# Packed values first, mixed weights copied out of PSUM, the value by halves of the heads, and another order of the block products in the last entry

## The chip, the cores and the metric

The kernel runs on one core of a Trainium2 chip. The metric is the time of one execution on the device in microseconds (us); lower is better. Before the change three runs took 408.6, 409.43 and 409.56 us.

## The reference, cut to what matters

Two softmax attentions over 8 batch entries (8 heads, 576 positions, head size 64, 32 packed queries), then a gated feed-forward block with a spatial matrix. All data is float32.

```
scale = 1.0 / np.sqrt(q.shape[-1])
def sm_attn(qq, kk, vv):                  # softmax(scale * qq @ kk^T) @ vv
    ...
p_packed = sm_attn(p, k, v)               # 32 packed rows per head
out = sm_attn(q, p_packed, p_packed)      # 576 rows per head
x = out with the heads side by side       # (8, 576, 512)
h = np.maximum(x @ w_in, 0.0)             # 1024 columns
u, v = h[..., :512], h[..., 512:]
v_n = (v - mean(v)) / np.sqrt(var(v) + 1e-06)
v_s = np.einsum('ts,bsd->btd', w_spatial, v_n) + b_spatial[None, :, None]
result = (u * v_s) @ w_out
```

## The kernel before

The eight batch entries are worked off one after the other; the code for entry 0 is written out by hand with the preparation of the weights, and entries 1 to 7 run through one loop over `b`, which is unrolled. The program order of every engine is the order of the code (all calls of TensorE, VectorE, ScalarE and GpSimd are pinned), so an instruction that waits holds up all behind it on its engine. Float32 products are made from a high and a low part (names ending in `_h`, `_l`): the high part is a copy on ScalarE, the low part a subtraction on VectorE, and TensorE adds three products.

PSUM is used as four quarters of two banks, `ps0` to `ps3`, through `on(q0)` to `on(q3)`; each stage takes the quarters in a written order, and a quarter can be written again once its reader is done. One entry on TensorE has these stages, in this order:

- `value(g)`: x @ w_in for the second half of the columns (the normalised half), in three groups of rows. The attention weights `a_h`, `a_l` are multiplied with the mixed weights `m_h[:, 1]`, `m_l[:, 1]` (packed values times w_in); `r` is the half of the heads (parity of the head).
- transposes of the packed weights of entry b+2 and of the packed values of entry b+1.
- `up(e)`: the first half of the columns, four groups.
- the mixing stage, small tiles of the array, work for later entries: `query_scores` (qT,ppT: scores of b+1), `mix(1)` and `mix(0)` (w_in_sb,ppT: mixed weights of b+1), `pack_values` (v_sb,p1T: packed values of b+2) and `pack_scores` (kT,pT: packed scores of b+3). VectorE takes the scores of b+1 out of PSUM by `query_spread`; `mix_hi` and `mix_lo` read the mixed weights in PSUM.
- `gate(e)`: the spatial matrix times the normalised half, four groups of 28 matmuls; `gated(e)` multiplies it into `u` on VectorE.
- `product`: the last matrix product in seven block products of 12 matmuls each (A11, S1, A12, S4, S3, S2, A22), with blocks T1 to T4 formed on VectorE from blocks of `u`. ScalarE makes the high parts (`block_hi`), VectorE the low ones (`block_lo`). P1, P5, P57 and U are sums kept in SBUF.

Between these VectorE and ScalarE run the softmax of entry b+1 (`query_max` to `query_tail`), whose weights the next `value` needs. The four output blocks of an entry are formed in tiles `o` (a pool of two buffers, which also holds `part` of `relu(2)`) and stored by DMAs that SyncE issues. Queue of the loads on SyncE: q of b+2, v of b+3, k of b+4, each behind the stage that read the buffer.

The quoted lines are the end of the last entry: VectorE forms the block 21 in two halves, then 22, each stored by its own DMA.

```
        ff.product(A22, "T4", onto=S3)
...
            for f in range(2):
                ff.out21(slice(f, f + 1))
            ff.out22()
```

## Time and profile before

| | |
|---|---|
| median of three runs | 409.43 us |
| profiled execution, its own time | 407.98 us |
| its span, first to last instruction | 406.2 us |
| busy: PE (matmul), DVE (VectorE), ACT (ScalarE), POOL (GpSimd) | 394.9, 332.9, 192.7, 74.1 us |
| granted TensorE clock, mean | 0.996 of full speed |

A busy PE is not PE at its peak: matmuls overlap, and their ends are modelled. How fast PE really goes is read from the starts of its rows in the timeline. In the trace all instructions carry one line (a helper's), so they are told apart by the names of their tiles: `qT,ppT`, `w_in_sb,ppT`, `v_sb,p1T` and `kT,pT` are the mixing stage, `m_h,a_h` is the value, `wsp` the gates, `wout` the block products.

### The profile page before, as it was taken

What the parts mean: (1) busy time and instruction counts of PE and PEld (TensorE: products, weight loads), DVE (VectorE), ACT (ScalarE), POOL (GpSimd) and SP (SyncE); (2) the same over time, 40 slices, a digit from 0 to 9 for tenths busy, and PEclk for the clock granted to TensorE, in tenths of its full rate; (3) what the DMA queues carried; (4) which work ended last, traced back from release to release, by engine and by line L of the source; (5) the groups of instructions that cost most, each with busy time, mean ns of one, the idle gap of its engine ahead of it and who ended that gap; (6) DMA issues with size and microseconds to landing.
All of it is one profiled execution on the core that took longest, in us unless ns stands there. A gap on an engine that the chain in (4) does not pass through costs nothing.

```text
span 406.2 us, 8936 instructions
## 1 busy us (share of the span) xinstructions
PE 394.9 (97%) x3800; PEld 354.5 (87%) x3800; DVE 332.9 (82%) x567; ACT 192.7 (47%) x291; POOL 74.1 (18%) x98
## 2 busy tenths in 40 slices
PE   7999999999999999999999999999999999999993
PEld 5768977799799879999699888999799889999993
DVE  2597799979799779977899788995899789978563
ACT  3587865766435353434634273244634272526140
POOL 1566445644000120002100030001200030004000
PEclk9999999999999999999999999999999999999998
DMA  7999057730810227020530205002300200020002
GB/s 306 382 383 397 20 178 305 241 116 2 293 66 31 87 81 278 2 85 34 224 129 31 87 13 225 0 29 89 120 0 30 87 2 2 0 102 17 2 30 88
DMA packets 16620, 46.62 MB, mean 115 GB/s; under 512 B 1346, under 2 KB 10562, under 8 KB 13764
## 3 DMA queue, kind: packets, MB, share of 16 engines
q1 hardware_dynamic: 16580, 46.05, 31.1%
q8 instruction: 30, 0.49, 0.5%
q14 instruction: 10, 0.08, 0.1%
HBM read 36.61 MB, written 9.44 MB: 113 GB/s over the span
## 4 chain that ended last, share of the span: by engine, by line
PE 94%; DVE 3%; POOL 1%; issue 1%; DMA 1%; POOLq 0%; DVEq 0%
PE ps_t L43 94%; DVE nmax L43 1%; POOL bits L43 1%; DMA out_t<-o 1%; DVE bits L43 0%; DVE t L43 0%; DVE o L43 0%; DVE sm_t L43 0%; DVE w_in_sb L43 0%; DVE pp L43 0%; DVE mx L43 0%; DVE prod L43 0%; POOL ident masks.py:199 0%; DVE rtot L43 0%; POOL ident masks.py:197 0%
## 5 line engine op out<-in xcount | busy, mean ns | idle before, releaser
L43 PE MATMUL ps_t<-wsp_h,v_h 128*128 128x288 f32 x256 | 55.9, 300 | 0.0
L43 PE MATMUL ps_t<-wsp_l,v_h 128*128 128x288 f32 x256 | 54.5, 295 | 0.0
L43 POOL TENSOR_TENSOR rstd<-mv,eps 128x2 f32<-128x2 f32 (+2 forms) x26 | 6.9, 265 | 245.5 <-DVE mv L43 245.4
L43 PE MATMUL ps_t<-t,wout_h 128*128 128x288 f32 x232 | 48.3, 294 | 0.0
L43 PEld LDWEIGHTS ps_t<-wsp_h,v_h 128*128 128x128 f32 x256 | 40.8, 188 | 3.8 <-DVE m_l L43 1.9
L43 PEld LDWEIGHTS ps_t<-wsp_l,v_h 128*128 128x128 f32 x256 | 41.5, 189 | 0.0
L43 ACT CAST g_h<-u 128x576 fp32r<-128x576 f32 x24 | 16.1, 674 | 49.4 <-DVE u L43 49.1
L43 PE MATMUL ps_t<-wsp_h,v_l 128*128 128x288 f32 x256 | 39.4, 296 | 0.0
L43 PEld LDWEIGHTS ps_t<-t,wout_h 128*128 128x128 f32 x232 | 38.0, 188 | 0.0
L43 PEld LDWEIGHTS ps_t<-wsp_h,v_l 128*128 128x128 f32 x256 | 35.9, 189 | 0.5 <-issue 0.5
L43 PE MATMUL ps_t<-t,wout_l 128*128 128x288 f32 x116 | 32.3, 294 | 0.0
L43 PE MATMUL ps_t<-g_h,wout_h 128*128 128x288 f32 x104 | 30.1, 305 | 0.6 <-DVE pp L43 0.6
L43 PE MATMUL ps_t<-g_h,wout_l 128*128 128x288 f32 x104 | 29.1, 295 | 0.0
L43 PE MATMUL ps_t<-a_h,m_h 128*128 128x288 f32 x128 | 28.1, 301 | 0.0
L43 PE MATMUL ps_t<-a_h,m_l 128*128 128x288 f32 x128 | 27.4, 296 | 0.0
L43 PE MATMUL ps_t<-a_l,m_h 128*128 128x288 f32 x128 | 27.4, 296 | 0.0
L43 DVE TENSOR_TENSOR u<-ps_t,u 128x576 f32<-128x576 f32 x28 | 21.0, 749 | 7.3 <-PE ps_t L43 7.3
L43 PE MATMUL ps_t<-m_l,a_h 128*128 128x512 f32 x80 | 25.8, 390 | 0.0
L43 PE MATMUL ps_t<-m_h,a_h 128*128 128x512 f32 x80 | 25.8, 391 | 0.0
L43 ACT ACTIVATE sm_t<-sm_t 128x576 f32<-128x576 f32 x16 | 11.0, 685 | 27.5 <-DVE sm_t L43 23.7
L43 DVE TENSOR_TENSOR o<-ps_t,prod 128x576 f32<-128x576 f32 (+1 forms) x15 | 10.7, 717 | 15.4 <-DMA out_t<-o 15.1
L43 ACT COPY part<-ps_t 64x512 f32<-64x512 f32 x8 | 4.7, 583 | 39.2 <-DVE o L43 39.2
(136 smaller groups left out, 989.6 us busy)
## 6 DMA issues: line engine op xcount, KB each, us to landing
out_t<-o SPq DMA_DIRECT2D x31, 288.0 KB, 2.3
v_sb<-in_v SPq DMA_DIRECT2D x8, 1024.0 KB, 8.1
qT<-in_q SPq DMA_DIRECT2D x7, 1152.0 KB, 5.4
kT<-in_k SPq DMA_DIRECT2D x7, 1152.0 KB, 8.4
raw<-in_w_in SPq DMA_DIRECT2D x4, 1024.0 KB, 12.7
raw<-in_w_out SPq DMA_DIRECT2D x2, 1024.0 KB, 9.8
kT<-in_k SPq DMA_DIRECT2D x2, 576.0 KB
qT<-in_q SPq DMA_DIRECT2D x2, 576.0 KB, 12.8
```

The lines of the kernel that those rows point to most:

```text
L43: return lambda *a, **k: self.tc.keep_in_program_order(call(*a, **k))
```

## The change

Four parts. (1) In the mixing stage `pack_values` and `packed` move ahead of `query_scores`, and the two `mix` follow each other. `mix_keep` copies each mixed-weight result whole from PSUM to SBUF (tile `kept`) on ScalarE, and `mix_hi` and `mix_lo` read the copy; `mix_lo(1)` moves behind the packed maxima of b+3. The load of v stands before that of q on SyncE. The quarters are dealt out anew. (2) `value(2)` and `value(0)` run by halves of the heads, first half of both, then second half of both. (3) The block products move to `down` and `last_down`. In `down` (entries 1 to 6) the products keep their order, and the work of VectorE and ScalarE between them is reordered: the sums and the scaling of the second softmax half (`query_sum(1)`, `query_norm(1)`) move from before the last gate into the products. Blocks 22 and 21 are formed in place in `prod` tiles (P57 and U) and stored from there. (4) `last_down` (entry 7) orders the products A11, S1, S2, S3, S4, A22, A12; the block 11 comes last, copied by ScalarE and stored in two halves.

```diff
@@ -487,6 +487,12 @@
                         True,
                     )
 
+        def mix_keep(self, x):
+            kept = two.tile([P, 2, FH], F32, tag="vn", name="kept")
+            act.copy(kept, self.ms[x])
+            self.ms[x] = kept
         def mix_hi(self, x, rs=slice(0, 2)):
             act.copy(self.m_h[:, x, rs, :], self.ms[x][:, rs, :])
 
@@ -510,7 +516,7 @@
         def chunks(self, g):
             return [c for c in (2 * g, 2 * g + 1) if c <= NC]
 
-        def value(self, g, psum=None, js=(0, 1), ns=(0, 1, 2)):
+        def value(self, g, psum=None, js=(0, 1), ns=(0, 1, 2), rs=(0, 1)):
             a_h, a_l, m_h, m_l = (getattr(self.att, x) for x in ("a_h", "a_l", "m_h", "m_l"))
             if g not in self.ps:
                 self.ps[g] = psum()
@@ -521,7 +527,7 @@
             if self.b == 0:
                 steps.sort(key=lambda rn: rn[1])
             for r, n in steps:
-                if n not in ns:
+                if n not in ns or r not in rs:
                     continue
                 aa, ww = terms[n]
                 for i in js[: len(self.chunks(g))]:
@@ -768,6 +774,12 @@
             act.copy(o, self.ds[k][:, :, :HS])
             self.put(o, f, t)
 
+        def out11_split(self):
+            o = self.out_block()
+            for i in range(2):
+                act.copy(o[:, i], self.ds[A12][:, i, :HS])
+                self.put(o, 0, 0, slice(i, i + 1))
         def out11(self):
             self.out_whole(A12, 0, 0)
 
@@ -776,16 +788,84 @@
             self.add_part(o, "U", S4)
             self.put(o, 0, 1)
 
-        def out21(self, fs=slice(0, 2)):
-            if fs.start == 0:
-                self.o21 = self.out_block()
-            self.add_part(self.o21, "U", A22, fs)
-            self.put(self.o21, 1, 0, fs)
+        def out21(self):
+            o = self.part("U")
+            self.add_part(o, "U", A22)
+            self.put(o, 1, 0)
 
         def out22(self):
-            o = self.out_block()
-            dve.tensor_tensor(o, self.part("U"), self.part("P57"), op=ALU.add)
+            o = self.part("P57")
+            dve.tensor_tensor(o, self.part("U"), o, op=ALU.add)
             self.put(o, 1, 1)
+        def down(self, turns, nxt):
+            self.product(A11, "g11", psum=on(turns[0]))
+            self.block_hi("g21")
+            self.block_sum("T3")
+            self.block_hi("T3")
+            self.block_lo("g21")
+            self.keep_part("P1", A11)
+            self.block_sum("T2")
+            self.block_hi("g22")
+            self.product(S1, "T1", psum=on(turns[1]))
+            self.block_lo("g22")
+            self.block_lo("T3")
+            self.block_hi("T2")
+            nxt.query_sum(1)
+            self.keep_part("P5", S1)
+            self.product(A12, "g21", onto=A11)
+            self.out11()
+            self.block_lo("T2")
+            nxt.query_norm(1)
+            self.block_sum("T4")
+            self.block_hi("T4")
+            self.product(S4, "g22", onto=S1)
+            nxt.query_turn(1)
+            nxt.query_hi(1)
+            self.product(S3, "T3", psum=on(turns[2]))
+            self.add_part("P57", "P5", S3)
+            self.block_lo("T4")
+            nxt.query_lo(1)
+            nxt.query_tail(1)
+            self.product(S2, "T2", psum=on(turns[3]))
+            self.add_part("U", "P1", S2)
+            self.out12()
+            self.product(A22, "T4", onto=S3)
+            self.out22()
+            self.out21()
+        def last_down(self, turns):
+            self.product(A11, "g11", psum=on(turns[0]))
+            self.block_sum("T2")
+            self.block_hi("T2")
+            self.block_sum("T3")
+            self.block_hi("T3")
+            self.block_lo("T2")
+            self.keep_part("P1", A11)
+            self.product(S1, "T1", psum=on(turns[1]))
+            self.block_hi("g22")
+            self.block_lo("T3")
+            self.block_lo("g22")
+            self.keep_part("P5", S1)
+            self.block_sum("T4")
+            self.block_hi("T4")
+            self.product(S2, "T2", psum=on(turns[3]))
+            self.add_part("U", "P1", S2)
+            self.block_hi("g21")
+            self.product(S3, "T3", psum=on(turns[2]))
+            self.block_lo("T4")
+            self.add_part("P57", "P5", S3)
+            self.block_lo("g21")
+            self.product(S4, "g22", onto=S1)
+            self.out12()
+            self.out22()
+            self.product(A22, "T4", onto=S3)
+            self.out21()
+            self.product(A12, "g21", onto=A11)
+            self.out11_split()
 
 
 
@@ -1109,8 +1189,9 @@
         att, nxt, far = nxt, far, further
         further = Attention(b + 3) if b + 3 < B else None
         ff = FeedForward(b, att)
-        ff.value(2, psum=on(q0))
-        ff.value(0, psum=on(q1))
+        for r in range(2):
+            ff.value(2, psum=on(q0), rs=(r,))
+            ff.value(0, psum=on(q1), rs=(r,))
         ff.relu(2)
         ff.value(1, psum=on(q2))
         ff.relu(0)
@@ -1146,42 +1227,45 @@
         ff.up(3, psum=on(q3))
         ff.up_relu(3)
         ff.norm_hi(1)
+        if far:
+            far.pack_values(on(q1))
+            far.packed()
+            if further:
+                load_v(b + 3)
         if nxt:
-            nxt.query_scores(psum=by_turns(q1, q2))
+            s0, s1, m1, m0 = (q2, q0, q3, q1) if far else (q1, q2, q0, q3)
+            nxt.query_scores(psum=by_turns(s0, s1))
             nxt.query_tiles()
             if far:
                 load_q(b + 2)
-            nxt.mix(1, psum=on(q0))
             nxt.query_spread(0)
+            nxt.mix(1, psum=on(m1))
+            nxt.mix_keep(1)
             nxt.query_spread(1)
+            nxt.mix(0, psum=on(m0))
+            nxt.mix_keep(0)
             nxt.mix_hi(1)
-            if far:
-                far.pack_values(on(q3))
-                far.packed()
-                if further:
-                    load_v(b + 3)
-            nxt.mix_lo(1)
         ff.norm_lo(1)
         if nxt:
-            nxt.mix(0, psum=on(q1))
-            nxt.mix_hi(0)
             if further:
-                further.pack_scores(psum=by_turns(q2, q3))
+                further.pack_scores(psum=by_turns(s0, s1))
                 if b + 4 < B:
                     load_k(b + 4)
                 for r in range(2):
                     further.pack_max(r)
                     further.pack_exp(r)
-            nxt.mix_lo(0)
+            nxt.mix_lo(1)
+            nxt.mix_hi(0)
             nxt.query_max(0)
             nxt.query_sub(0)
             nxt.query_exp(0)
+            nxt.mix_lo(0)
             if further:
                 further.pack_sum()
         if further:
-            turns = (q0, q1, q2, q3)
+            turns = (q3, q1, q2, q0)
         else:
-            turns = (q3, q2, q0, q1) if nxt else (q1, q2, q0, q3)
+            turns = (q2, q0, q3, q1) if far else (q1, q2, q0, q3)
         if not nxt:
             for cs in ((0, 1), (2, 3)):
                 ff.gate((0, 1), "hm", cs, psum=by_turns(*turns[:2]))
@@ -1207,48 +1291,11 @@
             elif nxt and e == 2:
                 nxt.query_lo(0)
                 nxt.query_tail(0)
-                nxt.query_sum(1)
-                nxt.query_norm(1)
...
+            ff.down(turns, nxt)
         else:
-            for f in range(2):
-                ff.out21(slice(f, f + 1))
-            ff.out22()
-        q0, q1, q2, q3 = turns[0], turns[1], turns[3], turns[2]
+            ff.last_down(turns)
+        q0, q1, q2, q3 = turns[0], turns[3], turns[1], turns[2]
 
 
 _INS = ["q", "k", "v", "vt", "p", "w_in", "w_sp", "b_sp", "w_out"]
```

On PE, mixing stage of entry 2, before (`ps` is a PSUM quarter; `x8` counts matmuls):

```order
L43 MATMUL ps2_t_1877<-qT_1331,ppT_1797 32x288 x8
L43 MATMUL ps0_t_1878<-qT_1331,ppT_1797 32x288 x8
L43 MATMUL ps1_t_1901<-w_in_sb_73,ppT_1797 32x512 x8
L43 MATMUL ps3_t_1915<-v_sb_1392,p1T_1784 32x64 x40
L43 MATMUL ps2_t_1963<-w_in_sb_73,ppT_1797 32x512 x8
L43 MATMUL ps0_t_1977<-kT_1431,pT_1429 32x288 x8
L43 MATMUL ps3_t_1978<-kT_1431,pT_1429 32x288 x8
```

The same place on PE in the changed kernel:

```order
L43 MATMUL ps1_t_1879<-v_sb_1354,p1T_1786 32x64 x40
L43 MATMUL ps2_t_1925<-qT_1377,ppT_1799 32x288 x8
L43 MATMUL ps0_t_1926<-qT_1377,ppT_1799 32x288 x8
L43 MATMUL ps3_t_1951<-w_in_sb_73,ppT_1799 32x512 x8
L43 MATMUL ps1_t_1964<-w_in_sb_73,ppT_1799 32x512 x8
L43 MATMUL ps2_t_1981<-kT_1433,pT_1431 32x288 x8
L43 MATMUL ps0_t_1982<-kT_1433,pT_1431 32x288 x8
```

The 40 matmuls of the packed values went from between the two mixes to the front.

On DVE, from the last gate to the block products of entry 2, before (`sm` sums and `sm_t` weights of the softmax, `u<-ps` the last `gated`, `u<-u` T3, `g` T2 and T4, `g_l` and `t` low parts, `at` a transpose):

```order
L43 TENSOR_REDUCE sm_2125<-sm_t_1912 128x18
L43 TENSOR_SCALAR sm_2125<-sm_2125 128x18
L43 RECIPROCAL sm_2125<-sm_2125 128x18
L43 TENSOR_TENSOR sm_t_1912<-sm_t_1912,sm_2125 128x576
L43 TENSOR_TENSOR u_1825<-ps3_t_2130,u_1825 128x576
L43 TENSOR_TENSOR u_1825<-u_1825 128x2x288
L43 TENSOR_TENSOR g_l_2082<-u_1825,g_h_2081 128x576
L43 TENSOR_TENSOR g_2084<-u_1825,g_2084 128x576
L43 TENSOR_TENSOR g_l_2082<-u_1825,g_h_2081 128x576
L43 TENSOR_TENSOR t_2194<-u_1825,t_2194 128x576
L43 TENSOR_TENSOR g_2216<-u_1825,g_2084 128x576
```

A later stretch on DVE in the changed kernel, from T2 (`g_2090`) to the low part of T4 (`t_2225`):

```order
L43 TENSOR_TENSOR g_2090<-u_1827,g_2090 128x576
L43 TENSOR_TENSOR g_l_2088<-u_1827,g_h_2087 128x576
L43 TENSOR_TENSOR t_2176<-u_1827,t_2176 128x576
L43 TENSOR_REDUCE sm_2201<-sm_t_1962 128x18
L43 TENSOR_SCALAR sm_2201<-sm_2201 128x18
L43 RECIPROCAL sm_2201<-sm_2201 128x18
L43 TENSOR_TENSOR t_2199<-g_2090,t_2199 128x576
L43 TENSOR_TENSOR sm_t_1962<-sm_t_1962,sm_2201 128x576
L43 TENSOR_TENSOR g_2223<-u_1827,g_2090 128x576
L43 STREAM_TRANSPOSE at_2239<-sm_t_1962 128x576
L43 TENSOR_TENSOR prod_2179<-ps2_t_2242,prod_2179 128x576
L43 TENSOR_TENSOR t_2225<-g_2223,t_2225 128x576
```

The sums and scaling of the softmax went from ahead of the last `gated` to behind the low part of T3; the low part of T4 now stands behind the transpose and P57.

On SP, the stores of the last entry before (`o_4736` is block 11, `o_4785` block 12, `o_4800` block 21, `o_4805` block 22):

```order
L764 DMA out_t<-o_4736 128x2x288
L764 DMA out_t<-o_4785 128x2x288
L764 DMA out_t<-o_4800 128x288 x2
L764 DMA out_t<-o_4805 128x2x288
L1301 UNCONDITIONAL_BRANCH
```

And in the changed kernel (`o_4782` block 12, `prod_4715` block 22, `prod_4716` block 21, `o_4813` block 11):

```order
L770 DMA out_t<-o_4782 128x2x288
L770 DMA out_t<-prod_4715 128x2x288
L770 DMA out_t<-prod_4716 128x2x288
L770 DMA out_t<-o_4813 128x288 x2
L1348 UNCONDITIONAL_BRANCH
```

Block 11 went from first to last, in halves.

## Rows read from the trace of the kernel before

**Rows 1.** Chain of waits that ended last, in order of time: start us, us, what

```profile
74.13 324.15 PE ps_t L43 x2922
...
399.87 2.26 DMA out_t<-o
```

**Rows 2.** Timeline of PE, mixing stage of entry 2: start us, us, instruction [idle before]

```profile
147.47 1.23 PE L43 MATMUL ps_t<-qT,ppT 64*32 64x288 f32 x32
148.46 1.27 PE L43 MATMUL ps_t<-w_in_sb,ppT 64*32 64x512 f32 x16
149.66 1.68 PE L43 MATMUL ps_t<-v_sb,p1T 128*32 128x64 f32 x76
151.13 0.63 PE L43 MATMUL ps_t<-w_in_sb,ppT 64*32 64x512 f32 x4
...
152.07 1.38 PE L43 MATMUL ps_t<-kT,pT 64*32 64x288 f32 x32
153.38 0.53 PE L43 MATMUL ps_t<-wsp_h,v_h 128*128 128x288 f32 x2
```

**Rows 3.** Timeline of PE, mixing stage of entry 6, which has no packed values

```profile
332.45 2.18 PE L43 MATMUL ps_t<-w_in_sb,ppT 64*32 64x512 f32 x32
334.56 0.53 PE L43 MATMUL ps_t<-wsp_h,v_h 128*128 128x288 f32 x2
```

**Rows 4.** Timeline of PE, mixing stage of entry 3, from scores to first gate

```profile
193.81 1.83 PE L43 MATMUL ps_t<-qT,ppT 64*32 64x288 f32 x28
...
200.39 0.40 PE L43 MATMUL ps_t<-wsp_h,v_h 128*128 128x288 f32 x1
```

**Rows 5.** Timeline of DVE, block 21 of entry 2

```profile
184.71 0.76 DVE L43 TENSOR_TENSOR o<-ps_t,prod 128x576 f32<-128x576 f32 x1 [4.10 <-DMA out_t<-o]
```

**Rows 6.** Timeline of ACT, three `up_relu` of entry 3, the first on the second scores' quarter

```profile
194.02 1.70 ACT L43 ACTIVATE u<-ps_t 128x576 f32<-128x576 f32 x3
```

**Rows 7.** Timeline of PE, block products of entry 2: A11, S1, A12, next value

```profile
168.40 0.30 PE L43 MATMUL ps_t<-g_h,wout_h 128*128 128x288 f32 x1
...
169.98 0.29 PE L43 MATMUL ps_t<-t,wout_h 128*128 128x288 f32 x1
...
171.65 0.40 PE L43 MATMUL ps_t<-g_h,wout_h 128*128 128x288 f32 x1
...
179.77 0.40 PE L43 MATMUL ps_t<-m_h,a_h 128*128 128x512 f32 x1
```

**Rows 8.** Timeline of DVE, entry 2: `mix_lo(0)`, `query_sum(1)`, last `gated`, T3, T2, low part

```profile
155.64 1.22 DVE L43 TENSOR_TENSOR m_l<-ps_t,m_h 128x1024 fp32r<-128x1024 f32 x1
...
167.63 0.75 DVE L43 TENSOR_REDUCE sm<-sm_t 128x18 f32<-128x576 f32 x1
...
169.60 0.75 DVE L43 TENSOR_TENSOR u<-ps_t,u 128x576 f32<-128x576 f32 x1
170.39 0.76 DVE L43 TENSOR_TENSOR u<-u 128x576 f32<-128x576 f32 x1
...
171.77 0.75 DVE L43 TENSOR_TENSOR g<-u,g 128x576 f32<-128x576 f32 x1
172.44 0.75 DVE L43 TENSOR_TENSOR g_l<-u,g_h 128x576 fp32r<-128x576 f32 x1
```

**Rows 9.** Timeline of ACT, entry 2: `mix_hi(1)`, high part of g21, P1

```profile
149.77 1.01 ACT L43 CAST m_h<-ps_t 128x1024 fp32r<-128x1024 f32 x1 [0.61 <-PE ps_t L43]
...
170.39 0.68 ACT L43 CAST g_h<-u 128x576 fp32r<-128x576 f32 x1 [4.16 <-DVE u L43]
170.97 0.63 ACT L43 COPY prod<-ps_t 128x576 f32<-128x576 f32 x1
```

**Rows 10.** Timeline of PE, the last two matmuls of the program

```profile
399.41 0.43 PE L43 MATMUL ps_t<-t,wout_h 128*128 128x288 f32 x2
```

**Rows 11.** Timeline of DVE, block 22 of the last entry

```profile
402.23 0.76 DVE L43 TENSOR_TENSOR o<-prod 128x576 f32<-128x576 f32 x1 [1.53 <-DMA out_t<-o]
```

**Rows 12.** DMA issues between 399.8 and 401.3 us: KB each, median us to landing

```profile
out_t<-o SPq DMA_DIRECT2D x2, 144.0 KB, 2.2
```

More of the change, by code (lines that the diff above doesn't have):

```diff
@@ L1209, in body @@
                 nxt.query_tail(0)
-                nxt.query_sum(1)
-                nxt.query_norm(1)
-        ff.product(A11, "g11", psum=on(turns[0]))
-        ff.block_hi("g21")
-        ff.block_sum("T3")
-        ff.block_lo("g21")
-        ff.keep_part("P1", A11)
-        ff.block_hi("g22")
-        ff.block_sum("T2")
-        ff.product(S1, "T1", psum=on(turns[1]))
-        ff.block_hi("T3")
-        ff.block_lo("g22")
-        ff.keep_part("P5", S1)
-        ff.block_lo("T3")
-        ff.block_hi("T2")
-        ff.product(A12, "g21", onto=A11)
-        ff.out11()
-        ff.block_sum("T4")
-        ff.block_lo("T2")
-        ff.block_hi("T4")
-        ff.product(S4, "g22", onto=S1)
-        ff.block_lo("T4")
-        if nxt:
-            nxt.query_turn(1)
-            nxt.query_hi(1)
-        ff.product(S3, "T3", psum=on(turns[2]))
-        ff.add_part("P57", "P5", S3)
-        if nxt:
-            nxt.query_lo(1)
-            nxt.query_tail(1)
-        ff.product(S2, "T2", psum=on(turns[3]))
-        ff.add_part("U", "P1", S2)
-        ff.out12()
-        ff.product(A22, "T4", onto=S3)
-        if nxt:
-            ff.out22()
-            ff.out21()
-        else:
-            for f in range(2):
-                ff.out21(slice(f, f + 1))
-            ff.out22()
-        q0, q1, q2, q3 = turns[0], turns[1], turns[3], turns[2]
+        if nxt:
+            ff.down(turns, nxt)
+        else:
+            ff.last_down(turns)
+        q0, q1, q2, q3 = turns[0], turns[3], turns[1], turns[2]
 _INS = ["q", "k", "v", "vt", "p", "w_in", "w_sp", "b_sp", "w_out"]
```

## The prediction

> **What bounds the kernel now.** I read the chain of waits first: from 74 us on it stays on PE in one piece of 324.15 us, and leaves it only at the end, for a store [rows 1]. From entry 1 on, then, only three things cost time: PE's own pace, the places where PE stands, and what comes after its last matmul. Busy PE time hides short stands, so I went through PE's timeline stage by stage, by starts, and compared the same stage between entries. Two stages differ or lose. The mixing stage takes 153.38 - 147.47 = 5.91 us in entry 2 [rows 2], but 200.39 - 193.81 = 6.58 in entry 3 [rows 4]. The block products take 179.77 - 168.40 = 11.37 us, while 12 matmuls take 169.98 - 168.40 = 1.58, so seven products 11.06 [rows 7]: 0.3 is lost. Then I read DVE, ACT and the stores around these places.
>
> **Packed values first.** Two mixes in a row take 334.56 - 332.45 = 2.11 us up to the first gate [rows 3]; a mix ahead of the packed values takes 149.66 - 148.46 = 1.20 [rows 2]. If the second mix in entry 6 also takes 1.20 (it too is followed by matmuls over all 128 rows), the first one takes 0.91. Bringing the mixes together so saves 0.29 us in each of the five entries that have packed values (1 to 5). What the packed values cost ahead of the scores no row shows; ahead of a mix they take 151.13 - 149.66 = 1.47, and their next matmuls start while their last still run, so I keep 1.47. Bounds: nothing saved, if scores behind packed values lose the 0.29 again; or 0.58, if going from `up` to the packed values is as smooth as mix to mix. I take 5 x 0.29 = 1.45 us.
>
> **Stands in entry 3 and its like.** The scores run as two streams, one for each half of the rows, into two quarters. In entry 2 both start together. In entry 3 the second quarter is still read by ACT's `up_relu(1)`: it begins at 194.02, among three that take 1.70 [rows 6], that is 0.2 after PE's scores began [rows 4]. ACT is late because the normalisation on DVE is late, and that is because block 21 waited 4.10 us for a store to free its `o` tile [rows 5]. The change writes block 21 over U and block 22 over P57, so DVE no longer waits there; the tiles are next written (`v_h`, `v_l`) behind the whole value and most of `up`. In addition the scores now start 1.47 us later. Either would take away the stand, 6.58 - 5.91 = 0.67 us; entry 5 repeats the pattern. I take 2 x 0.66 = 1.32. If a store were still awaited, nothing is gained; a gain beyond this has no row.
>
> **Copies and order of quarters.** Twelve copies of 128x1024 go to ACT, about 1.01 us each, as its read of the same PSUM took [rows 9]. They stand where ACT waited for PE ahead of that read, and the first gate needs only the first copy: it ends about 1.0 us after the mix, and the second mix and the scores of b+3 (0.94 + 1.31 us, from 151.13 to 153.38 [rows 2]) cover it. Without that cover a copy would cost its 1.01 us on the first gate. The load of v goes ahead of that of q on SyncE, each about 1.5 to 2 us earlier or later for data needed one entry later (193.81 - 147.47 = 46 us [rows 2, 4]): nothing. GpSimd's order is the same. The value by halves asks for the second half's weights six matmuls later: it costs nothing and gives DVE time.
>
> **DVE in the products.** This is where the change costs. `mix_lo(1)` (1.22 us [rows 8]) moves behind the packed maxima, while the sums and scaling of the second softmax half, 169.60 - 167.63 = 1.97 us, move behind T3's low part. Before, the last `gated` began 1.20 us after the first product matmul (169.60 against 168.40 [rows 7, 8]); now DVE is there in time, and `gated` starts when its gate is finished, which I put at 0.2 us. From then on, with 0.67 us a step (171.77 to 172.44) and 0.79 where a step reads the result before it (169.60 to 170.39) [rows 8]; ACT steps 0.58 [rows 9]; times from the first product matmul:
>
> - T3 0.99, low g21 1.70, T2 2.37. ACT: high g21 0.98, high T3 1.77, P1 2.35, high g22 2.93, ready 3.6. DVE stands 0.5.
> - low g22 3.62, low T3 4.29, the softmax sums 4.96 to 6.2, low T2 6.2, scaling 6.87, T4 7.54, transpose 8.21, P57 8.88, low T4 9.55, ready 10.3.
> - PE reaches A22, the seventh product, at 6 x 1.58 = 9.48; its first four matmuls need only the high part, its low part is needed at 9.48 + 0.53 = 10.0. **PE stands 0.3 us.**
> - Low part of the second attention half 10.22, its tail 11.0, U 11.1, ready 11.9. PE begins the value at 7 x 1.58 + 0.3 = 11.36; `value(0)` now goes to the quarter that U reads and starts two matmuls later, near 11.8: 0.1 us.
>
> Stage: 11.06 + 0.3 + 0.1 = 11.46 against 11.37. The stand before A12 (171.65 - 169.98 - 1.58 = 0.09, and what follows it) makes room for one before A22. I take +0.1 us in six entries: +0.6. Bounds: -0.3 an entry if DVE and ACT are a few tenths quicker, and as much more as DVE is later.
>
> **The end.** PE's last matmul ends at 399.41 + 0.43 = 399.84 [rows 10]; the span ends at 406.2, 6.4 us later. In between block 22 waits for a tile until 402.23 [rows 11], is ready at 402.99, lands about 2.26 later (as the store in [rows 1]), and about 0.95 of closing remains. Now everything but block 11 is done by then: with S2 and U early, DVE has only block 21 behind A22, one product (1.58 us) before the end. ACT copies block 11 in two halves, together between 0.63 [rows 9] and twice that; I take 0.75, and 0.15 for the second issue. A store of 144 KB takes 2.2 us [rows 12]. So the end comes 0.9 + 2.2 + 0.95 = 4.05 us after the last matmul: 2.3 us saved. If the two halves have to queue behind the three 288 KB blocks stored in the last 2 us, I allow one more half of 2.3 us, 1.2 saved; at best 2.6. The order of the products themselves leaves PE no stand there: the low part of T2 is ready 2.5 us after `gated`, before S2 needs it at 3.16 + 0.53, T4's low part about 7.1 before 7.92, g21's about 8.5 before 9.5.
>
> **Sum.** -1.45 - 1.32 + 0.6 - 2.3 = -4.47 us. The profiled execution took 407.98 us (span 406.2 and 1.8 around it), so it would take 403.5. The median of the runs is 409.43, 1.45 above that execution; I forecast for the median: 409.43 - 4.47 = **405.0 us**, with its own range of 404.0 to 406.0.
>
> **Rivals.**
>
> - DVE keeps up in the products, and PE loses nothing there: 6 x 0.4 us better, 402.6. For it: DVE's stand of 0.5 us hangs on the order of four ACT steps. Against: the late low part is the result of 14 steps in a row.
> - The mixing stage gets no shorter, since packed values to scores costs what mix to packed values cost: 405.0 + 1.45 = 406.4. For it: no row shows that sequence. Against: packed values to mix runs on without a gap [rows 2]. The Trainium skill (TensorEngine Tiling (Array Packing), Key Properties) says that a change of the tiling mode drains TensorE; by it the change from packed values to scores would be paid as well, and the time would be this rival's. The trace so far shows such a price for mix to packed values (1.20 against 0.91) and none for packed values to mix.
> - The stores collide at the end: 405.0 + 1.2 = 406.2. For it: four blocks leave in the last microseconds where two did. Against: 144 KB beside a larger store took no longer than usual [rows 12].
> - The freed wait comes back elsewhere, so that entries 3 and 5 stand as before: 406.3.
> - Slower: DVE falls behind from the gates on, because `mix_lo(1)` now stands behind the maxima and ACT's copies delay `mix_hi(0)` and so `mix_lo(0)`. Each 0.1 us that the low part of T4 is later than 10.3 costs 0.1 in each of six entries. It loses against before from 4.47 / 6 = 0.75 us, and visibly from (4.47 + 1.2) / 6 = 0.95; DVE would have to be some 1.4 us later at the last gate, since it arrives there about 0.5 early by my steps. 410.7. Nothing in the profile speaks for so much; ACT is idle for more than half of the span.
>
> **Chances.** Forecast 0.45, DVE keeps up 0.2, mixing no shorter 0.14, stores collide 0.09, wait comes back 0.04, slower 0.08 (a small part of it within 0.3%). Times from 402.6 to 408.0 hold the cases of one sign and half of a combination of two losses. A difference under 0.3% (1.2 us) is what a measurement of this kernel can't tell from none. Faster by more than that, below 408.2: 0.87; same 0.07; slower 0.06.
>
> **What would show it.** On PE in entry 2: packed values, scores, mix, mix, scores of b+3, together near 5.6 us, and the same in entry 3; the matmul of T4's low part late by some 0.3; the stage of the products near 11.4; no DVE wait for a store. At the end: ACT's two copies right behind PE, two stores, and the span ending about 4 us after the last matmul. Wrong would be a product stage over 11.9 us, scores that start late behind the packed values, or an end more than 5 us behind PE.

## The result and the profile after

The changed kernel takes 403.67 us (median of four runs, 403.61 to 404.21) against 409.34 us before (four runs, 408.6 to 409.56). The ratio is 0.9868, with an interval of 0.985 to 0.9885: 1.3% less time, small but clear of the noise. The forecast was 405.0 us, its range 402.6 to 408.0.

The chain of waits of the changed kernel (start us, us, what) stays on PE in one piece, as in [rows 1], and now leaves it for ScalarE's copy instead of VectorE's wait for a store:

```profile
87.58 311.19 PE ps_t L43 x2864
398.80 0.40 ACT o L43
399.20 0.30 ACTq L1348
```

PE's timeline of the changed kernel, the mixing stage of entry 2 and its first and last row in entry 3 (start us, us, instruction), answers to [rows 2, 4]:

```profile
147.82 1.73 PE L43 MATMUL ps_t<-v_sb,p1T 128*32 128x64 f32 x80
149.37 1.20 PE L43 MATMUL ps_t<-qT,ppT 64*32 64x288 f32 x32
150.34 2.13 PE L43 MATMUL ps_t<-w_in_sb,ppT 64*32 64x512 f32 x32
152.06 1.38 PE L43 MATMUL ps_t<-kT,pT 64*32 64x288 f32 x32
153.37 0.40 PE L43 MATMUL ps_t<-wsp_h,v_h 128*128 128x288 f32 x1
...
193.94 1.73 PE L43 MATMUL ps_t<-v_sb,p1T 128*32 128x64 f32 x80
...
199.49 0.40 PE L43 MATMUL ps_t<-wsp_h,v_h 128*128 128x288 f32 x1
```

Read by starts, the stage takes 153.37 - 147.82 = 5.55 us, and 5.55 in entry 3 too: no stand is left there.

PE's block products of entry 2 (A11, S1, A12, S4, A22's first matmul with T4's low part, and the value behind them), to be held against [rows 7]:

```profile
168.40 0.29 PE L43 MATMUL ps_t<-g_h,wout_h 128*128 128x288 f32 x1
...
169.98 0.29 PE L43 MATMUL ps_t<-t,wout_h 128*128 128x288 f32 x1
...
171.57 0.34 PE L43 MATMUL ps_t<-g_h,wout_h 128*128 128x288 f32 x1
...
173.22 0.38 PE L43 MATMUL ps_t<-g_h,wout_h 128*128 128x288 f32 x1
...
178.68 0.63 PE L43 MATMUL ps_t<-t,wout_h 128*128 128x288 f32 x3
...
179.81 0.40 PE L43 MATMUL ps_t<-m_h,a_h 128*128 128x512 f32 x1
```

The stage takes 11.41 us instead of 11.37. By starts the seven products take 1.59, 1.58, 1.65, 1.69, 1.61, 1.61 and 1.68 us, where 1.58 is full pace; the last, A22, spends 0.21 us instead of 0.13 from its first matmul with T4's low part to the next. VectorE in that stretch: the last `gated`, g22's low part, T4's low part ([rows 8] before):

```profile
168.60 0.76 DVE L43 TENSOR_TENSOR u<-ps_t,u 128x576 f32<-128x576 f32 x1 [0.39 <-PE ps_t L43]
...
172.06 0.76 DVE L43 TENSOR_TENSOR g_l<-u,g_h 128x576 fp32r<-128x576 f32 x1 [0.53 <-ACT g_h L43]
...
177.85 0.74 DVE L43 TENSOR_TENSOR t<-g,t 128x576 fp32r<-128x576 f32 x1
```

VectorE is now in time at the last `gated` (it waits 0.39 us for PE there) and stands 0.53 us for g22's high part. ScalarE's copies of P1 and P5, which free the quarters that A12 and S4 add to:

```profile
170.82 0.63 ACT L43 COPY prod<-ps_t 128x576 f32<-128x576 f32 x1
...
172.50 0.64 ACT L43 COPY prod<-ps_t 128x576 f32<-128x576 f32 x1
```

They end at 171.45 and 173.14, just as A12 (171.57) and S4 (173.22) are due. That is where PE first loses its pace.

The end: ScalarE's two copies, and the last two stores in the table of DMA issues (KB each, median us to landing), against [rows 10 to 12]:

```profile
398.80 0.70 ACT L43 COPY o<-ps_t 128x288 f32<-128x288 f32 x2 [4.48 <-PE ps_t L43]
```

```profile
out_t<-o SPq DMA_DIRECT2D x2, 144.0 KB, 1.8
```

PE's last matmul ends at 398.76 and the span at 402.4: 3.64 us, where it was 406.2 - 399.84 = 6.36.

### The profile page after: what moved, and what is told of

Its sections match the earlier page's. It is cut to its first block, busy times and chain, and to the rows that moved or that the text cites. A ratio compares the mean times of both kernels' runs of the same rounds, so it can differ in the third digit from the quotient of the medians.

```text
span 402.4 us, 8926 instructions
## 1 busy us (share of the span) xinstructions
PE 393.5 (98%) x3800; PEld 357.3 (89%) x3800; DVE 332.1 (83%) x566; ACT 204.2 (51%) x304; POOL 74.2 (18%) x98
## 4 chain that ended last, share of the span: by engine, by line
PE 90%; DVE 5%; DMA 2%; POOL 1%; issue 1%; SPq 0%; ACT 0%; ACTq 0%; POOLq 0%; DVEq 0%
PE ps_t L43 90%; DMA raw<-in_w_in 2%; DVE sm L43 1%; DVE sum L43 1%; POOL bits L43 1%; DVE m_l L43 1%; DVE sm_t L43 1%; DVE bits L43 0%; DVE nmax L43 0%; DVE t L43 0%; POOL a_l L43 0%; DVE w_in_sb L43 0%; SPq L112 0%; DVE at L43 0%; DVE mx L43 0%
## 5 line engine op out<-in xcount | busy, mean ns | idle before, releaser
L43 PE MATMUL ps_t<-t,wout_h 128*128 128x288 f32 x232 | 49.5, 298 | 0.0
L43 ACT CAST t<-g 128x576 fp32r<-128x576 f32 x21 | 14.2, 675 | 24.5 <-DVE g L43 23.8
L43 ACT ACTIVATE vr<-ps_t 128x1024 f32<-128x1024 f32 (+1 forms) x18 | 16.7, 932 | 19.1 <-PE ps_t L43 19.1
```

The source lines that it names most:

```text
L43: return lambda *a, **k: self.tc.keep_in_program_order(call(*a, **k))
```

## The experiments

Eleven kernels. The table has the stage lengths in us, by differences of starts in PE's timeline, for entry 2 (the value is the one that follows), and for the last entry's products and the time from PE's last matmul to the end of the span (the span is given to 0.1 us, so this time is good to 0.05). Products at full pace take 11.07. Ratios are to the runs of the kernel before on the same chip beside them (their medians are 408.4 to 409.3; one is shown).

| kernel | mixing | products | value | last products | end | median (range, runs) | ratio to before, interval |
|---|---|---|---|---|---|---|---|
| before | 5.91 | 11.37 | 6.36 | 11.23 | 6.36 | 408.82 (407.13 to 410.78, 29) | |
| tail_only | 5.91 | 11.36 | 6.37 | 11.43 | 3.70 | 407.11 (405.16 to 409.32, 12) | 0.9959, 0.9939 to 0.9979 |
| in_place_only | 5.91 | 11.36 | 6.37 | 11.23 | 6.36 | 407.54 (406.61 to 407.96, 12) | 0.9964, 0.9949 to 0.9979 |
| mixing_only | 5.55 | 11.86 | 6.37 | 11.23 | 6.33 | 411.00 (409.01 to 413.86, 12) | 1.0049, 1.0028 to 1.0070 |
| old_interleave | 5.55 | 11.86 | 6.36 | 11.42 | 3.72 | 407.53 (406.71 to 408.04, 12) | 0.9977, 0.9963 to 0.9991 |
| old_mixing | 5.91 | 11.35 | 6.45 | 11.43 | 3.63 | 405.48 (404.77 to 407.16, 6) | 0.9937, 0.9913 to 0.9961 |
| changed kernel | 5.55 | 11.41 | 6.45 | 11.42 | 3.64 | 403.67 (403.61 to 404.21, 4) | 0.9868, 0.9850 to 0.9885 |
| value_whole | 5.55 | 11.40 | 6.37 | 11.41 | 3.72 | 404.38 (403.25 to 405.64, 5) | 0.9902, 0.9877 to 0.9926 |
| no_copies | 8.53 | 11.35 | 6.42 | 11.37 | 3.76 | 422.22 (one) | |
| down_mended | 5.55 | 11.71 | 6.36 | 11.23 | 3.94 | 405.61 (405.29 to 405.82, 6) | 0.9918, 0.9894 to 0.9942 |
| down_again | 5.55 | 11.07 | 6.36 | 11.23 | 3.88 | **401.31** (401.22 to 401.63, 4) | 0.9827, 0.9805 to 0.9849 |
| values_between | 5.91 | 11.06 | 6.37 | 11.23 | 3.84 | 404.28 (404.02 to 405.50, 6) | 0.9906, 0.9886 to 0.9925 |
| own_blocks | 5.55 | 11.07 | 6.36 | 11.23 | 3.93 | 402.54 (401.94 to 402.81, 5) | 0.9857, 0.9836 to 0.9879 |

### The end alone: tail_only

The kernel before; its last entry alone gets the new order of products, the additions in place and the store by halves.

```diff
...
-            for f in range(2):
-                ff.out21(slice(f, f + 1))
-            ff.out22()
+            ff.last_down(turns)
```

> The kernel before with the new order of the last entry alone (products A11, S1, S2, S3, S4, A22, A12; blocks 22 and 21 of this entry formed in place; block 11 last in two halves). My theory: the end after PE's last matmul falls from 6.4 us to about 3.7, less 0.2 that PE stands before A22, where P57 has to be read out of the quarter onto which A22 accumulates: 2.5 us, ratio about 0.994. Rival, the four stores that leave in the last microseconds collide: 1.2 us or less, ratio 0.997 or more.

Measured 0.9959, between what the theory and the rival gave. The end fell from 6.36 to 3.70 us as in the changed kernel, and the last products lost the same 0.2 us. The gain in the runs is smaller than these 2.5 us, 1.7; the profiled execution shows a loss in entry 6 to 7, where VectorE waits for a store longer than in the same place before (1.75 us):

```profile
365.28 0.76 DVE L43 TENSOR_TENSOR o<-ps_t,prod 128x576 f32<-128x576 f32 x1 [3.77 <-DMA out_t<-o]
```

Behind it the normalisation is late, and no mixing stage covers it: the last value takes 7.03 us, the gate 15.78 instead of 14.93.

### Blocks 22 and 21 in place alone: in_place_only

The kernel before; block 22 of entries 1 to 6 goes over P57, and block 21 over U.

```diff
+        def out22_in(self):
+            o = self.part("P57")
+            dve.tensor_tensor(o, self.part("U"), o, op=ALU.add)
+            self.put(o, 1, 1)
...
-            ff.out22()
-            ff.out21()
+            ff.out22_in()
+            ff.out21_in()
```

> The kernel before with blocks 22 and 21 of entries 1 to 6 formed in place and stored from there, nothing else. My theory: DVE no longer waits for a store (16.6 us in all before), and that takes the two stands of the scores away: 1.3 us, ratio about 0.997; no other stage changes. Rival, the wait of DVE is cover for nothing on PE: no change.

Measured 0.9964, as expected. PE in entry 3, first scores and first gate:

```profile
194.03 1.23 PE L43 MATMUL ps_t<-qT,ppT 64*32 64x288 f32 x32
...
199.94 0.53 PE L43 MATMUL ps_t<-wsp_h,v_h 128*128 128x288 f32 x2
```

The mixing stage takes 5.91 us in entry 3 as in entry 2, and 4.71 instead of 5.28 in entry 5: the stand of [rows 4] hangs on the store wait of [rows 5] and goes with it, without any change of order.

### The new mixing stage alone: mixing_only

The kernel before with the mixing stage, the copies and the order of quarters of the changed one; products, value, stores and end stay old.

```diff
+            far.pack_values(on(q1))
+            far.packed()
...
+            nxt.mix_keep(1)
...
+            nxt.mix_keep(0)
...
-            turns = (q0, q1, q2, q3)
+            turns = (q3, q1, q2, q0)
```

> The kernel before with the new mixing stage alone (packed values first, the two mixes together, whole copies, its new quarters); the old value, products, stores and end. My theory: the stage falls from 5.91 to 5.55 us in five entries, 1.8 us, and the stands in entries 3 and 5 go as well (1.3 us), because the scores start 1.5 us later though DVE still waits 4 us for a store: 3.1 us, ratio about 0.992. Rival, the stands need the freed store: only 1.8 us, ratio 0.9955. Second rival, the copies delay DVE and give some of it back in the products.

Measured 1.0049, 0.5% more time, with the whole interval above 1. The theory held in the stage: 5.55 us in entries 1 to 4, and no stand in entry 3, though VectorE waits 3.71 us for a store in entry 2. The second rival held in the time, and took more than it allowed: the products take 11.86. PE, VectorE and ScalarE at A12 of entry 2, three fences:

```profile
172.32 0.40 PE L43 MATMUL ps_t<-g_h,wout_h 128*128 128x288 f32 x1 [0.41 <-ACT prod L43]
```

```profile
170.27 0.75 DVE L43 TENSOR_TENSOR u<-ps_t,u 128x576 f32<-128x576 f32 x1
```

```profile
171.06 0.68 ACT L43 CAST g_h<-u 128x576 fp32r<-128x576 f32 x1 [4.16 <-DVE u L43]
171.63 0.63 ACT L43 COPY prod<-ps_t 128x576 f32<-128x576 f32 x1
```

The products start at 168.58, and the last `gated` begins 1.69 us later, where it was 1.20 in [rows 7, 8]. VectorE's work has not shrunk, only the stage above it. ScalarE waits for `gated` to cast g21, P1's copy stands behind that cast in its queue, and A12 waits 0.41 us for P1. The stage's 0.36 us is given back there with more. In the profile the last entry loses 1.8 us besides (value 7.34 us, gate 15.75), behind a store wait of 4.07 us, as in tail_only.

### The new mixing stage with the old interleave: old_interleave

The changed kernel with the products of entries 1 to 6 in the code order of before.

```diff
+                nxt.query_sum(1)
+                nxt.query_norm(1)
...
-            ff.down(turns, nxt)
+            ff.product(A11, "g11", psum=on(turns[0]))
+            ff.block_hi("g21")
+            ff.block_sum("T3")
+            ff.block_lo("g21")
...
```

> The changed kernel with the products of entries 1 to 6 interleaved with the rest as before (sums of query half 1 and their scaling ahead of VectorE's last gated addition, blocks' high and low parts in the old order); blocks 22 and 21 are still added in place. My theory, that the new mixing stage pays only because this work was moved behind the last gated addition: A12 waits for P1's copy again, products 11.85 us instead of 11.41, value 6.36 instead of 6.45, 0.35 more in each of six entries: 405.8 us. Rival, that the stores in place were what gave the mixing its gain back: 404.0 or less.

Measured 407.53, later than either theory had it. Products of 11.86, the length that my theory had, with the same wait at A12 and the second half's sums ahead of the last `gated` on VectorE:

```profile
172.03 0.40 PE L43 MATMUL ps_t<-g_h,wout_h 128*128 128x288 f32 x1 [0.41 <-ACT prod L43]
```

```profile
168.02 0.75 DVE L43 TENSOR_REDUCE sm<-sm_t 128x18 f32<-128x576 f32 x1
...
169.98 0.75 DVE L43 TENSOR_TENSOR u<-ps_t,u 128x576 f32<-128x576 f32 x1
```

The blocks are in place here, so stores are not what gave the gain back. In entries 3, 5 and 6 the products take 11.99, 12.12 and 12.14, more than I counted; by stages products and value lose 3.0 us against the changed kernel in the profiled executions. The medians differ by 3.9, and the last 0.9 has no stage that I could show.

### The old mixing stage with the new interleave: old_mixing

The changed kernel with the mixing stage of before.

```diff
-            far.pack_values(on(q1))
...
-            nxt.mix_keep(1)
...
-            nxt.mix_keep(0)
...
+                far.pack_values(on(q3))
...
+            nxt.mix(0, psum=on(q1))
...
-            turns = (q3, q1, q2, q0)
+            turns = (q0, q1, q2, q3)
```

> The changed kernel with the mixing stage of before (order, no copies, old quarters); the rest stays changed. It is the fourth corner beside in_place_only, old_interleave and the changed kernel. My theory: the mixing stage takes 5.91 us again, without stands, instead of 5.55, in five entries; products stay at 11.35 to 11.41: 405.5 us. Rival, that the new interleave does it all and the mixing stage nothing: 403.7. Other rival, that the interleave costs by itself where VectorE was not late (PE waits as P1 to P5 are copied later): products 11.6 or more, 406.7.

Measured 405.48, and 5.91 and 11.35 us in the stages: as expected. With in_place_only less the gain at the end (407.54 - 2.72 + 0.2 = 405.0, an estimate from the table) the four corners, each with the new end and blocks in place, are: neither 405.0, interleave alone 405.5, mixing stage alone 407.5, both 403.7. As far as the estimated corner goes, the two parts pay only together.

### The value whole: value_whole

```diff
-        for r in range(2):
-            ff.value(2, psum=on(q0), rs=(r,))
-            ff.value(0, psum=on(q1), rs=(r,))
+        ff.value(2, psum=on(q0))
+        ff.value(0, psum=on(q1))
```

> The changed kernel with value(2) whole and then value(0) whole, as before. The prediction's term is nothing: 403.5 to 403.8 us, value 6.40 to 6.45 us in each entry. Rival, that the halves cover a wait: a stand of 0.2 us or more in value per entry, 405 us or more.

Median 404.38, in neither's bounds, and its runs (403.25 to 405.64) lie around those of the changed kernel. The profile shows no stand in the value: 6.35 to 6.37 us in entries 2 to 7, up to 0.08 less than by halves. The halves cover no wait here. In the profiles they cost the changed kernel 0.33 us over the six entries, and nothing in down_again, whose products are done earlier; the runs are too far apart to tell.

### Without the copies: no_copies

```diff
-            nxt.mix_keep(1)
-            nxt.mix_keep(0)
```

> The changed kernel without the two copies of the mixed weights out of PSUM: high and low parts are taken from PSUM, as before, in the new order. If the copies are what lets the gate's first product start at once: its quarter stays taken until VectorE has the low part of mixed weights 1, 156.2 instead of 153.4 in entry 2, and 2.8 us stand in each of six entries, 420 us (some 3 of it taken up by slack on VectorE: 415 at the least). Rival, that the order alone does it: 404 us.

One execution, 422.22 us. PE's first gate of entry 1, and VectorE's low part that it waits for:

```profile
110.11 0.82 PE L43 MATMUL ps_t<-wsp_h,v_h 128*128 128x288 f32 x2 [2.91 <-DVE m_l L43]
```

```profile
108.75 1.21 DVE L43 TENSOR_TENSOR m_l<-ps_t,m_h 128x1024 fp32r<-128x1024 f32 x1
```

The wait is the expected one, 2.98 us a stage (4.29 from scores to gate instead of 1.31), but in four entries, not six: 11.9 us. The rest is a cost that I had not foreseen. The windows around the stand (stretch, us, PE busy with its instructions, granted clock, DMA share, GB/s), entry 1 and then entry 3:

```profile
107.10:110.11 3.01, 0.10 (x3) 0.87 1.05 405
110.11:115.00 4.89, 4.89 (x20) 0.50 0.77 317
115.00:120.00 5.00, 5.00 (x37) 0.88 0.01 3
...
213.10:228.10 15.00, 15.00 (x113) 1.00 0.26 109
```

Behind the stand of 2.91 us in entry 1 PE's granted clock is 0.50, the lower of its two levels (1.2 GHz), and the gate takes 17.42 us in entry 1, 17.59 in entry 2 and 16.50 in entry 4 instead of 15.03; in entry 3 the same stand cost no clock. That is 6.4 us. The sum was near because two errors met.

### The products' order mended: down_mended, then down_again

The changed kernel with other orders in `down` (first four hunks) and in `last_down` (the last). In down_mended the old copy of P5 stays as well.

```diff
             self.block_sum("T3")
+            self.keep_part("P1", A11)
             self.block_hi("T3")
             self.block_lo("g21")
-            self.keep_part("P1", A11)
...
-            self.block_lo("g22")
             self.block_lo("T3")
+            self.block_lo("g22")
+            self.keep_part("P5", S1)
             self.block_hi("T2")
             nxt.query_sum(1)
-            self.keep_part("P5", S1)
...
-            self.block_lo("T4")
             self.add_part("P57", "P5", S3)
+            self.block_lo("T4")
```

> The changed kernel with its products mended: P1 copied before the high part of T3 and P5 before that of T2 on ScalarE; the low part of T3 before that of g22 on VectorE (which stood 0.53 us there); in the last entry P57 before the low part of T4. My theory: the stage of the products falls from 11.41 to about 11.07 us and the value from 6.44 to 6.37 in six entries, and the last entry loses 0.2 less: 2.5 us faster than the changed kernel, about 401.2. Rival, the slower pace of PE in the products (0.134 instead of 0.132 us a matmul) is not from waits but from what the other engines and the stores do to it: no faster than the changed kernel, 403.7.

Measured 405.61: both expectations missed, by a slip of mine. The kernel copies P5 twice, and S4 waits for the second copy, ScalarE's third of these in the fence below:

```profile
174.08 0.40 PE L43 MATMUL ps_t<-g_h,wout_h 128*128 128x288 f32 x1 [0.36 <-ACT prod L43]
```

```profile
172.27 0.65 ACT L43 COPY prod<-ps_t 128x576 f32<-128x576 f32 x1
172.80 0.68 ACT L43 CAST t<-g 128x576 fp32r<-128x576 f32 x1
173.38 0.65 ACT L43 COPY prod<-ps_t 128x576 f32<-128x576 f32 x1
```

It still measures something: one ScalarE step too many ahead of S4 makes A12's start-to-start 2.11 us instead of 1.58. The value (6.36) and the last products (11.23) were mended already. Without the second copy:

> The changed kernel with four moves: in each entry before the last P1 is copied before T3's high part, P5 before T2's, and T3's low part comes before g22's; in the last entry P57 is added before T4's low part. It is the earlier kernel of this order without its second copy of P5, which S4 waited for (0.53 us an entry). My theory, that the products' small stands come from this order on ScalarE and VectorE: products 11.07 to 11.10 us instead of 11.41, value 6.36 instead of 6.45, in six entries, and 0.2 in the last: 2.8 us less, 400.9 us. Rival, that PE's slower pace has another cause: products stay at 11.3 or more, 402.5 us or more.

Measured 401.31 us, the fastest kernel of this study; 0.4 above what I expected. Of that, 0.2 is the last entry: its products are 0.19 us shorter, but its end is 0.24 longer. PE's products and ScalarE's copies of P1 and P5, entry 2:

```profile
167.39 0.29 PE L43 MATMUL ps_t<-g_h,wout_h 128*128 128x288 f32 x1
...
168.97 0.29 PE L43 MATMUL ps_t<-t,wout_h 128*128 128x288 f32 x1
...
170.56 0.29 PE L43 MATMUL ps_t<-g_h,wout_h 128*128 128x288 f32 x1
...
178.46 0.40 PE L43 MATMUL ps_t<-m_h,a_h 128*128 128x512 f32 x1
```

```profile
169.17 0.64 ACT L43 COPY prod<-ps_t 128x576 f32<-128x576 f32 x1
...
170.86 0.64 ACT L43 COPY prod<-ps_t 128x576 f32<-128x576 f32 x1
```

P1 is ready 0.75 us before A12 (169.81 against 170.56), and all seven products take 1.58 to 1.59: 11.07 us. What the changed kernel lost in products and value in entries 1 to 6 lay in the order of two copies and one low part; which of the three gives how much was not tested.

### The packed values between the mixes again: values_between

The kernel down_again with these lines (and the load of v behind them) moved from ahead of the scores to between the mixes, and two quarters exchanged:

```diff
-            s0, s1, m1, m0 = (q2, q0, q3, q1) if far else (q1, q2, q0, q3)
+            s0, s1, m1, m0 = (q2, q0, q3, q2) if far else (q1, q2, q0, q3)
...
             nxt.query_spread(1)
+            if far:
+                far.pack_values(on(q1))
+                far.packed()
...
             nxt.mix(0, psum=on(m0))
...
-                further.pack_scores(psum=by_turns(s0, s1))
+                further.pack_scores(psum=by_turns(q1, s1))
```

> The kernel down_again (401.3 us) with the packed values between the two mixing products, copies and all else kept (quarters of PSUM exchanged so that none is waited for). If it is the change between the forms of matmul that the new order saves: mixing stage 5.84 to 5.91 us instead of 5.55, in five entries, 402.8 to 403.1 us. Rival, that the gain came with the copies and not with the order: 5.55 to 5.60, 401.5 us or less.

Measured 404.28 us. The mixing stage takes 5.91 us in entries 1 to 4 with the copies kept and no stand, so the order is worth 0.36. PE in entry 2:

```profile
147.28 1.23 PE L43 MATMUL ps_t<-qT,ppT 64*32 64x288 f32 x32
148.27 1.27 PE L43 MATMUL ps_t<-w_in_sb,ppT 64*32 64x512 f32 x16
149.47 1.67 PE L43 MATMUL ps_t<-v_sb,p1T 128*32 128x64 f32 x76
...
153.19 0.53 PE L43 MATMUL ps_t<-wsp_h,v_h 128*128 128x288 f32 x2
```

The first mix takes 1.20 us up to the packed values again, where two mixes together take 1.72 in the changed kernel. Entry 5 adds a stand that this edit made (its gate waits for the second copy, as no scores lie between):

```profile
291.36 0.53 PE L43 MATMUL ps_t<-wsp_h,v_h 128*128 128x288 f32 x2 [1.20 <-ACT kept L43]
```

With it the stage is 1.40 longer there: 4 x 0.36 + 1.40 = 2.84, of 2.97 measured.

### Own output blocks again: own_blocks

The kernel down_again; in entries 1 to 6 block 22, and block 21 likewise, has a block of its own.

```diff
...
-            o = self.part("P57")
-            dve.tensor_tensor(o, self.part("U"), o, op=ALU.add)
+            o = self.out_block() if self.b < B - 1 else self.part("P57")
+            dve.tensor_tensor(o, self.part("U"), self.part("P57"), op=ALU.add)
```

> The kernel down_again (401.3 us) with blocks 22 and 21 of entries 1 to 6 added into output blocks of their own again, which wait for an earlier store. If this wait is what spreads the runs of before and costs time: VectorE waits 3 to 4 us for a store before block 22 in most entries, the median is 402.5 us or more, and the runs lie over 2 us or more instead of 0.4. Rival, that the wait lies behind the value stage, where VectorE has nothing late: 401.3 us, runs within 0.5.

Measured 402.54: 1.2 us for the store wait, as expected, but runs 0.87 apart, not 2. VectorE in entry 2, and PE's mixing stage of entry 3 (first and last row):

```profile
183.78 0.76 DVE L43 TENSOR_TENSOR o<-ps_t,prod 128x576 f32<-128x576 f32 x1 [3.83 <-DMA out_t<-o]
```

```profile
192.79 1.73 PE L43 MATMUL ps_t<-v_sb,p1T 128*32 128x64 f32 x80
...
198.34 0.53 PE L43 MATMUL ps_t<-wsp_h,v_h 128*128 128x288 f32 x2
```

Six such waits, 12.6 us in all, and most are hidden: in the profile the transposes behind this one take 1.44 us instead of 1.12, entry 6's mixing stage 3.17 instead of 3.05, and entry 7's gate 15.27 instead of 14.93, 0.8 us together. The mixing stage of entry 3 behind this wait takes 5.55 us, without a stand.

## Why the prediction was right, and where it was not

From the first value of entry 1 to the end of the span the profiled executions take 406.2 - 86.99 = 319.2 us before and 402.4 - 87.58 = 314.8 after: 4.4 less, where the sum was 4.47. That they lie so near is luck in part: the errors of the terms go both ways.

| term | predicted | measured | from |
|---|---|---|---|
| packed values first, stands of entries 3 and 5 | -2.77 | -2.86 | entries 1, 2, 4: 0.36 each; 6.58 to 5.55; 5.28 to 4.58; entry 6: 0.05 |
| products and value, entries 1 to 6 | +0.6 | +0.98 | products 0.65, value 0.33 |
| products of the last entry | 0 | +0.20 | 11.23 to 11.42 |
| after the last matmul | -2.3 | -2.72 | 6.36 to 3.64 |

- **Packed values first** is right in cause (values_between) and in entries 1 to 4 a little small: 0.36 instead of 0.29. Entry 5 gained only 0.13 (4.71 us in in_place_only to 4.58), where I counted all five alike. The rival that the stage gets no shorter is out. It drew on a sentence of the Trainium skill (TensorEngine Tiling (Array Packing), Key Properties) that a change of the tiling mode drains TensorE. I read this stage wrongly there: the packed values run in two forms by turns and end in the form of scores and mixes, as these rows of the changed kernel show (the last packed values, then the first scores):

```profile
149.24 0.32 PE L43 MATMUL ps_t<-v_sb,p1T 64*32 64x64 f32 x8
149.37 0.47 PE L43 MATMUL ps_t<-qT,ppT 64*32 64x288 f32 x8
```

So there is no change of form from packed values to scores that could be paid; from `up` to the gate the form changes six times before and five after, and the sentence speaks for a gain. The change that is saved is the one the traces show: a mix ahead of packed values takes 1.20 us against 0.86 (half of 1.72). That every change costs the same they do not show: entry 5 saves one too.
- **The stands** go by the freed store wait alone (in_place_only, 1.2 us instead of 1.32). The prediction gave two reasons, either enough. The second, the later scores, suffices as well: in mixing_only and own_blocks VectorE waits 3.71 and 3.83 us for a store in entry 2, and the mixing stage of entry 3 takes 5.55.
- **The copies cost nothing**: right, and no_copies shows what their absence costs.
- **DVE in the products** is the step that failed in its place, though its sum was near. I put one stand of 0.3 us before A22's low part. T4's low part is ready at 178.59 - 168.40 = 10.19, close to the 10.3 of my steps, but PE reaches A22 0.25 us later than I had it, and loses only 0.1 there. It had lost the 0.25 at A12 and S4, whose quarters P1 and P5 free just in time, and to a pace of 0.134 us a matmul instead of 0.132. My list of steps had P1's copy in it, but I never held its end against A12's start. down_again shows it: with the copies earlier, nothing is lost.
- **Slower**: the mechanism of that rival, VectorE late at the last `gated`, is real. It took place in mixing_only and old_interleave, and `down` is what keeps it away. Most of the lateness (0.36 of 0.49 us in mixing_only) is the shorter stage itself, which the rival did not name; 0.13 is VectorE later in its own work.
- **The end**: right in size; the stores landed in 1.8 us, not 2.2. What I had wrong is "leaves PE no stand there": A22 adds to S3's quarter, which P57 must have read. VectorE ends that at 395.20, and A22 starts at 395.35 instead of about 395.24. The move of P57 in down_again takes the 0.2 us out of the products, but the end grows from 3.64 to 3.88 us, as its last two stores take longer to land (the same row as above):

```profile
out_t<-o SPq DMA_DIRECT2D x2, 144.0 KB, 2.0
```

From the last entry's first product to the end of the span every kernel with the new end takes 15.1 to 15.2 us, whether its products take 11.23 or 11.43: the 0.2 us cost the program nothing. What else sets the end was not tested; in down_again's last 3.5 us with stores (394.9 to 398.4) the DMA engines are busy 0.89 of the time, so the four blocks queue more than I had it, at no price to the forecast.
- **From profile to median**: the forecast was 1.3 us too high because I carried the offset of one execution over. The one of before was 1.4 us under its median, that of after 0.5 over. The store wait is no missing term: the 1.3 us that in_place_only gains in the runs are the stands of entries 3 and 5, which the sum has, and in own_blocks the stages show 0.8 of the 1.2 us.

Left open: why PE keeps the pace of 0.134 through S3 and S2, and why the runs of some kernels lie up to 4.9 us apart. With blocks of their own they spread most (before 3.7, mixing_only 4.9, tail_only 4.2), in place mostly 0.4 to 1.5; but value_whole and old_mixing are in place and spread 2.4, and own_blocks only 0.9.

## What to carry to other kernels

A stage made shorter on the bounding engine brings the next stage nearer to the engines that feed it: work out their arrival there before the gain is booked, and move their work in the same edit. For every product that accumulates onto a used quarter, hold the end of the copy that frees it against the product's start; where both fall within 0.1 us, the order of a few instructions on the feeding engines can be worth more than a large edit (here 2.4 us). Before a stand on PE is mended at the end of a program, look at what the end hangs on: here 0.2 us of it were worth nothing.

## What the runs showed of the hardware

- A stand of 2.9 us on PE (no_copies) was followed by a lower granted clock in three entries of four (0.50, that is 1.2 GHz, in the stretch shown), which cost 1.5 to 2.6 us on top of the stand; one of 1.2 us (values_between, entry 5) cost nothing, and the gate behind it took 15.02 us.
- PE ran two products (S3 and S2 of the changed kernel, entry 2, 1.61 us each) at 0.134 us a matmul of 288 columns instead of 0.132 without a wait between their matmuls; the cause is open.
- A mix takes 1.20 us when packed values follow and 0.86 when another mix follows (values_between and the changed kernel, entry 2).
- Stores of 144 KB at the end of the program landed in 1.8 us (changed kernel) and 2.0 us (down_again).
